# Last x tile of each later chunk turned by the DMA queue, and values, scores and global rows moved between the output steps

## The chip, the cores and the metric

The kernel runs on one core of a Trainium2 chip. The metric is device time in microseconds (us) for one execution. Engines are named as in the profile: PE is TensorE (PEld its weight loads), DVE is VectorE, ACT is ScalarE, POOL is GpSimd, SP is SyncE, whose queue issues most of the DMAs.

## The reference

Windowed attention with eight global positions, followed by a gated feed-forward layer (FFN) with a gated residual. In short:

```python
# q, k, v: (8 batches, 8 heads, 576 positions, 64); global_idx: 8 positions
scores = q @ k.T / sqrt(64)
keep   = (abs(pos_i - pos_j) <= 32) | is_global[i] | is_global[j]
attn   = softmax(where(keep, scores, -1e9))
x      = (attn @ v) laid out as 4608 tokens x 512      # heads side by side

g   = x @ w_gate                                       # 512 -> 1536
val = x @ w_val                                        # 512 -> 1536
ffn = (gelu(g) * val) @ w_out                          # 1536 -> 512
out = x + sigmoid(x @ w_res) * ffn                     # 4608 x 512, float32
```

## The kernel before

**Chunks.** The 4608 tokens are worked on as nine chunks `c` = 0 to 8 of 512 tokens. A chunk is eight attention windows of 64 queries (`CH = 8`), and its x has four tiles of 128 tokens, `t` = 0 to 3. A window sees 128 neighbouring keys and, besides, the global ones; queries that are themselves global are worked out apart, for all keys of a batch ("global rows"). A batch has nine windows, so a chunk can reach over two batches.

**One chunk's FFN.** For a chunk c > 0, PE first runs the twelve input steps (`ffn_in`, L614, through `ffn_steps`): for each of twelve blocks of 128 hidden units four matmuls into `g_ps` and four into `v_ps` (both L630), all with the turned x, `xt[c % 2]`, as the moving operand over all 512 tokens at once. ACT takes the GELU (L636), DVE multiplies (L639) into `ht`. So the first g of a chunk reads all four tiles of its turned x.

Then come sixteen output steps, `work_f`, four for each tile t (`ffn_out`): a gate (four matmuls into `r_ps`, L656, and a Tanh on ACT, L664), and three thirds of the twelve matmuls with `w_out` into `f_ps` (L686). The third one ends with `prb` on DVE (L690), `ob` on POOL (L692) and the output DMA on SP (L694). Steps are counted from 0: gate 0 is step 0, its thirds 1 to 3, gate 1 is step 4, and so on to 15.

**The next chunk's attention lies between these steps.** The order is written by hand: `jobs[n]` (L936 to L952) holds what is emitted in front of output step n, and the loop at the end of the kernel emits the jobs and then the step. Each engine and each queue keeps the order in which its instructions were emitted; waits come from the data and from the tile pools' buffers. For chunk c + 1 the jobs are:

- `global_exp` (step 0) and `global_rows` (step 4): the exponentials of the global scores on ACT, then matmuls into `sn` (L507, L510) and their masking into `vgs` on DVE (L514). Chunk 8 has none of this, since its batch, the last, was dealt with for chunk 7.
- `scores` in two halves, `half(0)` at step 1 and `half(1)` at step 4: 32 small matmuls (L534) on 64 rows of the array, four exponentials on ACT (L541) into `pt`; the masks on DVE (L557) are emitted at steps 1, 6 and 7.
- `values(c + 1, t)` at steps 5, 7, 9 and 11: sixteen matmuls with `pt` into `nd` (L575), two or four more for the global keys (L587), then on DVE a reciprocal `rden` (L599) and a product (L600) that writes x as tokens, `xtok`.
- `turn_x(c + 1, t)` at steps 7, 9, 11 and 13, in front of the step's other jobs: it turns one tile of `xtok` into `xt`. For chunks from 2 on, tiles 0 to 2 go by a DMA that transposes, issued on SP (L606); tile 3 goes by four matmuls with an identity into a PSUM tile `tx` (L610) and a copy by DVE (L611). Chunks 0 and 1 turn all tiles on PE.

**PSUM.** Three pools share its eight banks: `psm` with four buffers of a bank (g, v, r, f and half of the scores), `pss` with two (the other half of the scores, `tx`, turned globals), and `psn` with one buffer of two banks, which `sg` (global scores), `sn` and every `nd` use in turn.

**Queues.** SP's own order in these steps, before the change, is out 0, turn 0, out 1, turn 1, turn 2, out 2, out 3, and then for the next chunk the transposes of queries and keys. POOL issues the loads of queries, keys and values of later batches between its `ob`.

Of the kernel before, what the change touches and what calls it, by code (L numbers as in the profile page):

```python
# [16 lines left out]
def view(t, p0, pn, off, dims):  # L17

    step = t.ap[0][0]
    return bass.AP(tensor=t.tensor, offset=t.offset + p0 * step + off, ap=[[step, pn]] + dims)  # L20
# [3 lines left out]
def kernel(  # L24
# [460 lines left out]
    def global_exp(b, sg, ss):  # L485
        e = b % 2
        to = ptg[e].rearrange("k c r -> k (c r)")
        done = 0
        for part in ss:
            n = part.shape[1]  # L490
            nc.scalar.activation(to[:, done:done + n], part, ACTF.Exp, bias=0.0, scale=SCALE)
            done += n
        g = gt[e][:, 64:64 + S]
        nc.scalar.activation(g.rearrange("p (a c) -> p a c", a=2), sg[:, :, 0:288], ACTF.Exp, bias=0.0, scale=SCALE)
        nc.vector.tensor_tensor(g, g, maskr, ALU.mult)

    def global_rows(b):

        e = b % 2
        if b:  # L500
            sn = psn.tile([128, 2, 512], F32, name="sn", tag="nd")[:, 0, 0:2 * VG]
        else:
            sn = pss.tile([128, 2 * VG], F32, name="sn", tag="sc")
        for c in range(-1, 5):
            for p in range(NP):
                if c < 0:
                    nc.tensor.matmul(sn[32 * p:32 * p + 32, :], own[e][:, 32 * p:32 * p + 32],  # L507
                                     view(vgb, 0, 128, (b // 2) * VG, [[0, 2], [1, VG]]), start=True, stop=False)
                else:
                    nc.tensor.matmul(sn[32 * p:32 * p + 16, :], ptg[e][:, c, 16 * p:16 * p + 16],  # L510
                                     ve[e][:, c, 2 * p:2 * p + 2, :], start=False, stop=(c == 4))
        n = NP if b else NP // 2
        for p in range(0, NP, n):
            nc.vector.tensor_tensor(view(vgs, 0, 128, e * H * VG + 2 * VG * p, [[2 * VG, n], [VG, 2], [1, VG]]),  # L514
                                    view(sn, 0, 128, 0, [[0, n], [VG, 2], [1, VG]]),
                                    view(head8, 0, 128, 2 * p, [[2, n], [1, 2], [0, VG]]), ALU.mult)
# [27 lines left out]
    def scores(c, quad, pps=(0, 1)):  # L544

        i0 = (CH * c + 4 * quad) % NW
        banks = []
        for pp in pps:
            pool, tag = (psm, "mm") if pp else (pss, "sc")
            sc = [pool.tile([128, 2, 4, 64], F32, name="sc", tag=tag) for _ in range(2)]  # L550
            heads(c, quad, pp, sc, True)
            banks += [(pp, u, sc[u]) for u in range(2)]
        mine = [weigh(quad, *which, stay=(c == 1)) for which in banks]

        def mask(n0, n1):
            for m, x in mine[n0:n1]:
                nc.vector.tensor_tensor(m, x, view(maskw, 0, 128, 64 * i0, [[0, 2], [64, 4], [1, 64]]), ALU.mult)  # L557
        return mask

    def split(c, t):  # L560
        return c == 0 and t % 2 == 0

    def local_values(c, t):
        if split(c, t):
            nds = [psm.tile([128, 512], F32, name=f"nd{hf}", tag="mm") for hf in range(2)]
            nd = None
        else:
            nd = psn.tile([128, 2, 512], F32, name="nd", tag="nd")
            nds = [nd[:, 0, :], nd[:, 1, :]]
        wins = [divmod(CH * c + 2 * t + e, NW) for e in range(2)]  # L570
        for h in range(H):
            for e, (b, i) in enumerate(wins):
                vw = ve[b % 2][:, i // 2, h, :] if i % 2 == 0 else vo[b % 2][:, i // 2, h, :]
                c0 = (h * CH + 2 * t + e) * 128 - 64 * e
                nc.tensor.matmul(nds[h // 4][:, VG * (h % 4):VG * (h % 4) + VG],  # L575
                                 view(pt, 0, 128, c0, [[1, 128]]), vw, start=(h % 4 == 0 and e == 0), stop=False)
        return nd, nds, wins

    def values(c, t, begun=None):
        nd, nds, wins = begun or local_values(c, t)  # L580
        if wins[0][0] == wins[1][0]:
            parts = [(wins[0][0], 64 + 64 * wins[0][1])]
        else:
            parts = [(wins[0][0], S), (wins[1][0], 0)]
        for hf in range(2):
            for n, (b, c0) in enumerate(parts):
                nc.tensor.matmul(nds[hf][:, 0:HV], gt[b % 2][:, c0:c0 + 128], vgs[:, b % 2, HV * hf:HV * hf + HV],  # L587
                                 start=False, stop=(n == len(parts) - 1))
        rden = work.tile([128, H], F32, name="rden", tag="rden")
        if split(c, t):  # L590
            for hf in range(2):
                num = nds[hf][:, 0:HV].rearrange("p (h e) -> p h e", e=VG)
                nc.vector.reciprocal(rden[:, 4 * hf:4 * hf + 4], num[:, :, D])
                nc.vector.tensor_tensor(xtok[0][:, t, 256 * hf:256 * hf + 256].rearrange("p (h d) -> p h d", d=D),
                                        num[:, :, 0:D], view(rden, 0, 128, 4 * hf, [[1, 4], [0, D]]), ALU.mult)
            return
        num = nd[:, :, 0:HV].rearrange("p a (h e) -> p a h e", e=VG)
        r2 = rden.rearrange("p (a h) -> p a h", a=2)
        nc.vector.reciprocal(r2, num[:, :, :, D])  # L599
        nc.vector.tensor_tensor(xtok[c % 2][:, t, :].rearrange("p (a h d) -> p a h d", a=2, d=D),  # L600
                                num[:, :, :, 0:D], view(rden, 0, 128, 0, [[4, 2], [1, 4], [0, D]]), ALU.mult)

    def turn_x(c, t):
        mine = xt[c % 2][:, :, 128 * t:128 * t + 128]
        if c > 1 and t < 3:
            nc.sync.dma_start(mine, xtok[c % 2][:, t, :], transpose=True)  # L606
            return
        tx = pss.tile([128, NKT, 128], BF16, name="tx", tag="sc")
        for kk in range(NKT):
            nc.tensor.transpose(tx[:, kk, :], xtok[c % 2][:, t, 128 * kk:128 * kk + 128], ident)  # L610
        (nc.vector.tensor_copy if c or t == 3 else nc.scalar.copy)(mine, tx)  # L611
# [175 lines left out]

    values(0, 2)
    turn_x(0, 0)
    values(0, 3)  # L790
    turn_x(0, 1)
    begin(0, (0,))
    turn_x(0, 2)
    begin(0, (1,))
    begin(1)
# [11 lines left out]
    for c in range(NCH):  # L807
        b = c + 1
# [127 lines left out]
        jobs = {n: [] for n in range(16)}  # L936
        if c + 1 < NCH:
            if held is not None:
                jobs[0].append(lambda: global_exp(b, *held))
                jobs[4].append(lambda: global_rows(b))  # L940
            held_mask = {}

            def half(quad):
                held_mask[quad] = scores(c + 1, quad)

            jobs[1] += [lambda: half(0), lambda: held_mask[0](0, 4)]
            for t in range(4):
                jobs[5 + 2 * t].append(lambda t=t: values(c + 1, t))
                jobs[7 + 2 * t].insert(0, lambda t=t: turn_x(c + 1, t))
            jobs[4].append(lambda: half(1))  # L950
            jobs[6].append(lambda: held_mask[1](0, 2))
            jobs[7].append(lambda: held_mask[1](2, 4))  # L952
        for n in range(16):
# [32 lines left out]
```

The softmax here doesn't subtract the row's maximum and nothing guards it: scores larger than these inputs give would overflow.

## Time and profile before

| what | value |
|---|---|
| median of nine runs | 393.72 us (392.8 to 394.08) |
| the profiled execution's own time | 394.26 us |
| its span | 392.6 us |
| PE busy | 375.9 us, 96% of the span |
| DVE, ACT, POOL busy | 201.8, 170.2, 168.9 us |
| turns of x: by PE (L610) | 60 matmuls, 15 tiles |
| turns of x: by DMA (L606) | 21 transposes, 2.5 us from issue to landing at the median |

The profile shows one execution. A row of the timeline has the start in us from the span's start, the time from the first start to the last end, the engine, the line and the operation, the tile written and those read, the shapes, and how many instructions were merged; in square brackets stands how long the engine had been idle before it and what ended that. The ends of matmuls are modelled, and rows of PE overlap for that reason, so starts are compared. A few matmul records are missing, so a count can be one or two short. Landing is the time from a DMA's issue to its completion.

### The profile page before, as it was taken

To read this page: it belongs to the slowest core of one execution; us is meant where nothing else is said; L and a number is where in the kernel's file an instruction comes from. 1 tells how busy PE (TensorE), PEld (TensorE's weight loads), DVE (VectorE), ACT (ScalarE), POOL (GpSimd) and SP (SyncE) were. 2 spreads that over 40 slices of the span, in tenths; PEclk is the share of its full clock that TensorE was granted. 3 is DMA by queue.
4 is the path that set the end of the run, shared out by engine and by line. 5 is a ranking of instruction groups with operands and counts; after the bars stand their busy time and mean duration, and the time that the engine had idled before them with its cause. 6 is when DMAs were issued, how large, how long until landed. Compare 5 with 4: busy or idle time off the path is not lost.

```text
span 392.6 us, 8440 instructions
## 1 busy us (share of the span) xinstructions
PE 375.9 (96%) x3309; PEld 197.0 (50%) x3360; DVE 201.8 (51%) x446; ACT 170.2 (43%) x285; POOL 168.9 (43%) x203
## 2 busy tenths in 40 slices
PE   3989989999999999999999999999999999999996
PEld 2674555444644465445544554455445544554444
DVE  7766684436543664357444644655445534453422
ACT  6753783436333633354235533462338233723321
POOL 7787674858255424561466127712501210121012
PEclk9999999999999999999999999999999999999999
DMA  8999999699859913997299929993980210041002
GB/s 246 228 375 363 246 315 212 161 184 156 110 101 153 187 42 108 123 201 84 85 140 183 102 82 129 186 106 93 117 145 29 68 55 0 2 91 59 0 28 81
DMA packets 153002, 52.78 MB, mean 134 GB/s; under 512 B 136386, under 2 KB 143426, under 8 KB 152962
## 3 DMA queue, kind: packets, MB, share of 16 engines
q1 hardware_dynamic: 77024, 41.88, 44.2%
q0 software_dynamic: 75392, 9.84, 43.6%
q8 instruction: 26, 0.43, 0.5%
q10 hardware_dynamic: 546, 0.52, 0.4%
q14 instruction: 14, 0.11, 0.1%
HBM read 39.19 MB, written 9.44 MB: 124 GB/s over the span
## 4 chain that ended last, share of the span: by engine, by line
PE 71%; DMA 16%; POOL 4%; SPq 3%; issue 2%; DVE 2%; ACT 1%; ACTq 0%; DVEq 0%; POOLq 0%
PE f_ps L686 21%; PE v_ps L630 16%; PE g_ps L630 16%; PE r_ps L656 7%; PE nd L575 4%; DMA extra<-in_moe_w_val_dram 3%; SPq L185 2%; PE nd L587 2%; DMA wo_t<-in_k_dram 2%; PE sc L534 2%; DMA xt<-in_moe_w_gate_dram 2%; DMA xtok<-in_v_dram 2%; DMA kt<-k_st 2%; POOL ob L692 2%; DMA ht<-in_q_dram 2%
## 5 line engine op out<-in xcount | busy, mean ns | idle before, releaser
L639 DVE SCALAR_TENSOR_TENSOR ht<-gsb,v_ps 128x512 bf16<-128x512 bf16 x108 | 74.1, 687 | 94.9 <-PE v_ps L630 90.4
L636 ACT ACTIVATE gsb<-g_ps 128x512 bf16<-128x512 f32 x108 | 64.4, 597 | 122.7 <-PE g_ps L630 118.1
L692 POOL TENSOR_TENSOR ob<-prb,xtok 128x512 f32<-128x512 f32 x35 | 40.2, 1153 | 172.5 <-DVE prb L690 172.5
L630 PE MATMUL v_ps<-xt,wv_t 128*128 128x512 bf16 (+1 forms) x448 | 111.3, 368 | 0.7
L630 PE MATMUL g_ps<-xt,wg_t 128*128 128x512 bf16 (+1 forms) x445 | 110.7, 368 | 0.5
L686 PE MATMUL f_ps<-wo_t,ht 128*128 128x512 bf16 x402 | 96.6, 379 | 0.7
L630 PEld LDWEIGHTS <-wv_t 128*128 128x128 bf16 x456 | 43.5, 98 | 49.3 <-issue 0.4
L630 PEld LDWEIGHTS <-wg_t 128*128 128x128 bf16 x456 | 43.3, 98 | 49.4 <-issue 1.2
L686 PEld LDWEIGHTS <-ht 128*128 128x128 bf16 x420 | 40.0, 98 | 39.5
L664 ACT ACTIVATE rsb<-r_ps 128x512 bf16<-128x512 f32 x36 | 21.8, 608 | 67.0 <-PE r_ps L656 67.0
L690 DVE SCALAR_TENSOR_TENSOR prb<-rsb,f_ps 128x512 f32<-128x512 bf16 x35 | 24.0, 686 | 28.9 <-PE f_ps L686 26.4
L541 ACT ACTIVATE pt<-sc 128x512 bf16<-128x512 f32 x64 | 33.2, 619 | 9.6 <-PE sc L534 9.6
L656 PE MATMUL r_ps<-wr_t,xt 128*128 128x512 bf16 x130 | 35.6, 379 | 0.9
L91 POOL DMA_DIRECT2D q_st<-in_q_dram x25 | 21.4, 865 | 19.4 <-DMA qt<-q_st 19.1
L575 PEld LDWEIGHTS <-pt 128*128 128x128 bf16 x576 | 21.9, 97 | 9.3 <-PE r_ps L656 0.7
L557 DVE TENSOR_TENSOR pt<-pt,maskw 128x512 bf16<-128x512 bf16 x56 | 22.4, 421 | 7.1 <-ACT pt L541 5.8
L99 POOL DMA_DIRECT2D ve<-in_v_dram x30 | 25.5, 865 | 0.0
L600 DVE TENSOR_TENSOR xtok<-nd,rden 128x512 bf16<-128x512 f32 x34 | 23.5, 692 | 1.3
L575 PE MATMUL nd<-ve,pt 128*128 128x65 bf16 x320 | 22.4, 193 | 0.6 <-DVE xtok L600 0.6
L91 POOL DMA_DIRECT2D k_st<-in_k_dram x25 | 21.1, 871 | 3.6 <-DMA kt<-k_st 2.6
L599 DVE RECIPROCAL rden<-nd 128x8 f32<-128x8 f32 x34 | 7.0, 207 | 29.3 <-PE nd L587 29.3
L575 PE MATMUL nd<-vo,pt 128*128 128x65 bf16 x256 | 19.8, 193 | 0.4 <-PE r_ps L656 0.3
(174 smaller groups left out, 300.7 us busy)
## 6 DMA issues: line engine op xcount, KB each, us to landing
out_dram<-ob SPq DMA_DIRECT2D x35, 256.0 KB, 2.1
vo<-ve SPq DMA_DIRECT2D x12, 260.0 KB, 5.5
q_st<-in_q_dram POOLq DMA_DIRECT2D x20, 128.0 KB, 5.6
k_st<-in_k_dram POOLq DMA_DIRECT2D x20, 128.0 KB, 6.6
ve<-in_v_dram POOLq DMA_DIRECT2D x18, 128.0 KB, 6.5
wo_t<-in_k_dram SPq DMA_DIRECT2D x8, 256.0 KB, 6.6
vraw<-in_q_dram SPq DMA_DIRECT2D x8, 256.0 KB, 6.7
extra<-in_moe_w_out_dram SPq DMA_DIRECT2D x4, 512.0 KB, 6.9
```

The costliest lines, as they stand in the source:

```text
L91: nc.gpsimd.dma_start(dst[0:n, r, :].rearrange("p (h d) -> p h d", d=D), src[b].rearrange("h s d -> s h d")[128 * r:128 * r + n])
L99: nc.gpsimd.dma_start(t[p0:p1, c, :, 0:D], v[b].rearrange("h s d -> s h d")[s0 + p0:s0 + p1])
L541: nc.scalar.activation(sc if stay else mine, sc, ACTF.Exp, bias=0.0, scale=SCALE)
L575: nc.tensor.matmul(nds[h // 4][:, VG * (h % 4):VG * (h % 4) + VG], view(pt, 0, 128, c0, [[1, 128]]), vw, start=(h % 4 == 0 and e == 0), st ...
L600: nc.vector.tensor_tensor(xtok[c % 2][:, t, :].rearrange("p (a h d) -> p a h d", a=2, d=D), num[:, :, :, 0:D], view(rden, 0, 128, 0, [[4, ...
L630: nc.tensor.matmul(held[what][:, c0:c1], w[:, kk, 128 * j:128 * j + 128], x[:, kk, c0:c1], start=(kk == 0), stop=(kk == NKT - 1))
L636: nc.scalar.activation(held["s"], held["g"], ACTF.Gelu, bias=0.0, scale=1.0)
L639: nc.vector.scalar_tensor_tensor(ht[:, j, :], held["s"], 0.5, held["v"], ALU.mult, ALU.mult)
L656: nc.tensor.matmul(r_ps, xt[c % 2][:, kk, 128 * t:128 * t + 128], wr_t[:, kk, :], start=(kk == 0), stop=(kk == NKT - 1))
L686: nc.tensor.matmul(held["f"], ht[:, j, 128 * t:128 * t + 128], wo_t[:, j, :], start=(j == 0), stop=(j == NFF - 1))
L690: nc.vector.scalar_tensor_tensor(prb, held["r"], 1.0, held["f"], ALU.add, ALU.mult)
L692: nc.gpsimd.tensor_tensor(ob, prb, xtok[c % 2][:, t, :], ALU.add)
```

## The change

The last tile of x is turned by the DMA queue as well (for chunks from 2 on), and each turn is emitted right behind the values that it reads instead of in front of a later step. Values of tiles 0, 1 and 2 stay at steps 5, 7 and 9; those of tile 3 go from step 11 to step 10. The second half of the scores goes from step 4 to step 5, where it now stands behind the values and the turn of tile 0. The global rows go from step 4 to step 3.

```diff
     def turn_x(c, t):
         mine = xt[c % 2][:, :, 128 * t:128 * t + 128]
-        if c > 1 and t < 3:
+        if c > 1:
             nc.sync.dma_start(mine, xtok[c % 2][:, t, :], transpose=True)
             return
...
                 jobs[0].append(lambda: global_exp(b, *held))
-                jobs[4].append(lambda: global_rows(b))
+                jobs[3].append(lambda: global_rows(b))
...
             for t in range(4):
-                jobs[5 + 2 * t].append(lambda t=t: values(c + 1, t))
-                jobs[7 + 2 * t].insert(0, lambda t=t: turn_x(c + 1, t))
-            jobs[4].append(lambda: half(1))
+                n = (5, 7, 9, 10)[t]
+                jobs[n].append(lambda t=t: values(c + 1, t))
+                jobs[n].append(lambda t=t: turn_x(c + 1, t))
+            jobs[5].append(lambda: half(1))
             jobs[6].append(lambda: held_mask[1](0, 2))
             jobs[7].append(lambda: held_mask[1](2, 4))
```

On SP the order becomes out 0, turn 0, turn 1, out 1, turn 2, turn 3, out 2, out 3.

## The prediction

> **What bounds the kernel now.** I read the page from the top: busy shares, slices, the chain that ended last.
>
> ```profile
> PE 375.9 (96%) x3309; PEld 197.0 (50%) x3360; DVE 201.8 (51%) x446; ACT 170.2 (43%) x285; POOL 168.9 (43%) x203
> PE   3989989999999999999999999999999999999996
> PE 71%; DMA 16%; POOL 4%; SPq 3%; issue 2%; DVE 2%; ACT 1%; ACTq 0%; DVEq 0%; POOLq 0%
> ```
>
> PE is busy in every slice but the first and last, and no other engine is over 51%. So each microsecond added to PE's row of instructions, or put into it as a wait, lengthens the run. Next I read the timeline of PE, and of DVE and SP, for the sixteen output steps of one chunk (c=4; the values are those of chunk 5).
>
> ```profile
> 214.97 0.81 PE L656 MATMUL r_ps<-wr_t,xt 128*128 128x512 bf16 x3
> 215.92 0.64 PE L534 MATMUL sc<-qt,kt 64*128 64x64 bf16 x32
> 216.50 2.76 PE L686 MATMUL f_ps<-wo_t,ht 128*128 128x512 bf16 x12
> 219.19 0.24 PE L507 MATMUL sn<-vgb,own 128*32 128x130 bf16 x4
> ...
> 226.45 0.61 PE L587 MATMUL nd<-vgs,gt 128*128 128x260 bf16 x4
> 226.89 1.89 PE L686 MATMUL f_ps<-wo_t,ht 128*128 128x512 bf16 x8
> ...
> 231.05 0.39 PE L610 MATMUL tx<-ident,xtok 128*128 128x128 bf16 x4
> 231.28 2.75 PE L686 MATMUL f_ps<-wo_t,ht 128*128 128x512 bf16 x12
> 233.87 1.03 PE L630 MATMUL g_ps<-xt,wg_t 128*128 128x512 bf16 x4
> ```
>
> Each group starts where the one before it hands over: twelve f matmuls from 231.28 to 233.87 are 0.216 apiece, so one third of a tile (4) is 0.86 us. Nothing in these steps waits. The ends in the second column are modelled; I use starts.
>
> ```profile
> 227.09 0.21 DVE L599 RECIPROCAL rden<-nd 128x8 f32<-128x8 f32 x1 [0.46 <-PE nd L587]
> 227.34 0.69 DVE L600 TENSOR_TENSOR xtok<-nd,rden 128x512 bf16<-128x512 f32 x1
> 229.53 0.21 DVE L599 RECIPROCAL rden<-nd 128x8 f32<-128x8 f32 x1 [1.50 <-PE nd L587]
> ```
>
> This is the drain of the value bank `nd` of tile 2: PE hands over at 226.89, rden starts 0.20 later, xtok ends at 228.03, 1.14 after the hand-over. `nd` has one buffer only (pool `psn`), so tile 3's first value matmul can't start before that.
>
> **The change part by part.** The sum is made against the profiled execution, 394.26 us (span 392.6, 1.7 outside it); the median of the nine runs is 393.72, so I carry the difference over to that.
>
> *Tile 3's turn off TensorE.* Seven chunks (c=1 to 7 prepare chunks 2 to 8) lose four tx matmuls, 231.28 - 231.05 = 0.225 us of PE each: -1.57. DVE loses seven xt copies of 0.42 us and PSUM a tx tile; both were beside PE's work (DVE then waits 2.26 us for f), so nothing.
>
> *Tile 3's values one step earlier.* Tile 2 stays at step 9, tile 3 moves from 11 to 10, so between them on PE stands one third (0.86 us) where there were two (1.73). The bank needs 1.14 us plus the way from DVE back to PE. The early part of the trace has two places where PE did wait for this bank:
>
> ```profile
> 55.93 0.69 DVE L600 TENSOR_TENSOR xtok<-nd,rden 128x512 bf16<-128x512 f32 x1
> 56.73 0.19 PE L575 MATMUL nd<-vo,pt 128*128 128x65 bf16 x1 [0.27 <-PE r_ps L656]
> ...
> 62.31 0.69 DVE L600 TENSOR_TENSOR xtok<-nd,rden 128x512 bf16<-128x512 f32 x1
> 63.15 0.19 PE L575 MATMUL nd<-vo,pt 128*128 128x65 bf16 x1
> ```
>
> 56.62 to 56.73 and 63.00 to 63.15: 0.11 and 0.15 us; I take 0.13. Then tile 3 starts 1.27 after the hand-over instead of 0.86: a new wait of 0.405 us (0.385 to 0.425). The other chunks repeat it (c=1: hand-over 105.02, xtok ends 106.16). Behind the waiting matmul stands all of PE; nobody else has work for it. Seven times: +2.8. DVE is free when tile 2 is handed over (idle 0.23 to 0.46 us before its rden), with prb of tile 1 ahead of it in both orders, so the drain isn't longer than now.
>
> *The second half of the scores from step 4, in front of the gate, to step 5, behind values of tile 0; global rows from step 4 to 3.* The amount of PE work is the same; what changes is how often neighbours have different array shapes. Gate 0 should hand over at 214.97 + 4 x 0.216 = 215.83, sc starts at 215.92; f at 219.09, sn starts at 219.19: 0.09 to 0.10 us per change of shape. Before, sn, sc and the gate follow one another: into sn, sn to sc, sc to gate, three changes. After, sn stands alone between two thirds and sc alone between values and a third: four. The way out of sn into f is not in the trace; it lies between 0 and the 0.10 of the other changes, and I take 0.10, since leaving sc costs as much as entering it. Six chunks have global rows: +0.6 (0 to 0.6).
>
> Do the moved pieces find their inputs? Global rows would start near 218.3; the last exponential that they need ends at 216.1. The values of tile 0 need vgs: DVE is through with the first masks at 219.05, so vgs ends near 219.75, values start near 220.5. The second exponentials start 0.44 after their scores and take 2.06 us; the masks that use them come behind xtok of tile 0 and of tile 1 as now, and tile 2's values start some 4 us after these scores. These cost nothing; the cover is 0.7 us and more.
>
> Chunk 8 (c=7) has no global rows, and its exponentials come late, behind a table load:
>
> ```profile
> 338.73 4.03 ACT L541 ACTIVATE pt<-sc 128x512 bf16<-128x512 f32 x8
> ...
> 339.36 1.90 DVE L557 TENSOR_TENSOR pt<-pt,maskw 128x512 bf16<-128x512 bf16 x4 [2.64 <-ACT pt L541]
> ```
>
> The last mask of the first half ends at 341.26. Values of tile 0 would now come right behind gate 1, at 340.74 instead of 341.71; their eleventh matmul needs that mask and waits some 0.33 us. Against it, now the second half's scores lose 0.10 and gate 1 0.17 us on exponentials, which goes. Net +0.06 (-0.27 to +0.35).
>
> *The queues.* SP's order was out 0, turn 0, out 1, turn 1, turn 2, out 2; it becomes out 0, turns 0 and 1, out 1, turns 2 and 3, out 2. Turn 1 no longer stands behind out 1. POOL's order does not change.
>
> ```profile
> 227.89 0.35 SPq L694 DMA_DIRECT2D out_dram<-ob  x1
> 228.34 2.62 SPq L606 DMA_TRANSPOSE xt<-xtok  x2
> ...
> DMA to landing us min/median/max: 2.4/2.5/5.0
> ```
>
> Turn 2 issues at 228.34 as turn 1 does now, 1.2 us long. Tile 3's values start near 228.16, take 0.71, and xtok ends 1.14 later, near 230.0: turn 3 issues at 230.05 and by the median lands at 232.5. The next chunk's g, its first reader, would start at 233.87 + 0.405 - 0.225 = 234.05. So the landing has 4.0 us from its issue; 2.5 fits, and this step costs nothing. Without that cover, at 5.0, it costs 1.0 in that chunk. Out 2 has its ob near 232.6 and isn't held up. SP's next key and query loads hang on out 3, which moves with PE.
>
> Here the Trainium skill speaks against the change. In VectorE: DVE Perf Modes, sections "The three transpose paths" and "Rules for kernel authors", it says to turn a 128x128 block on TensorE where PSUM will do as the destination, and gives 390 ns for that and 1309 ns for the crossbar DMA. By its figure four blocks one behind the other would land 5.2 us after issue, an estimate by which seven chunks would wait about 1.2 us each and the run would come to 404. The trace disagrees on both: four blocks are 0.225 us of PE, and all four land 2.4 to 2.5 us after issue at the median.
>
> *Sum.* c=1 to 6: 0.405 - 0.225 + 0.10 = 0.28, times 6 is 1.7. c=7: 0.405 - 0.225 + 0.06 = 0.24. Together +1.9: 396.2 for an execution like the profiled one, 395.6 on the median.
>
> **The rivals.** *Late landings on top.* Of the 19 landings of x tiles that the trace can tell, three took 4.0 us or more, one 5.0. Two of these already touch the next chunk's start: at 274.46 and 354.53 its first g comes 0.1 and 0.05 us late, just behind a turn's landing at 274.32 and 354.40. A tile turned 0.3 to 0.5 later has less room. One such landing in seven chunks adds up to 1.0, two add 2: 396.6 to 397.6, here 396.9. For it: those rows. Against it: 16 of 19 land with over a microsecond left.
>
> *The bank wait is short, and the run gets faster.* All hangs on tile 3's wait, w: the sum is 7w - 1.57 + 0.6 + 0.06, zero at w = 0.13 us. If PE were free to go on (w = 0), the run would be 0.9 faster, 392.8. For it: 0.225 us of PE is certainly gone in each chunk, and no row of this stage shows a wait for the bank. Against it: the drain of 1.14 is read in every chunk, and one third is 0.86.
>
> *In between.* With w from 0.02 to 0.24 the result stays within 0.2% (0.8 us, about what a measurement of this kernel can tell from no change); the like follows if leaving sn is free and later waits take something up. PE's waits after 93 us that could do this (0.2 for kt at 214.85, those before g) are some 0.6 together: 395.0 at least, so that alone does not reach it. Middle 394.2.
>
> **How the numbers follow.** Forecast 0.65, late landings 0.18, in between 0.10, faster 0.07. The first two are slower: 0.83. Predicted: 395.6. Bounds: w at 0.385, no cost for leaving sn and the low end of c=7 give +0.8 to +1.1, so 394.6 below; late landings in one or two chunks 397.2 above. That leaves out the faster case, most of the one in between and a tail of the late one.
>
> **What the changed profile would show.** L610 with 32 matmuls instead of 60, L606 with 28 transposes instead of 21. In each chunk, PE idle some 0.4 us before the first nd of tile 3, put down to DVE xtok; tx gone between gate 3 and f; sn between two groups of f, with some 0.1 us on either side; turn 3 issued about 4 us before the next g. The prediction is wrong if PE goes from the third to tile 3's nd without a gap, if g waits for L606 in most chunks, or if tile 0's values wait for vgs.

## The result, and the profile after

The changed kernel takes 395.12 us at the median of nine runs (394.57 to 395.39). The kernel before has a median of 393.72 over the 29 runs it is compared with. The ratio is 1.0035, with a 95% interval from 1.0026 to 1.0043: slower by 1.0 to 1.7 us. The profiled execution took 395.16 us, 393.4 of it the span.

The page of the changed kernel, with the lines that were read first on the page before:

```profile
PE 375.9 (96%) x3281; PEld 195.0 (50%) x3332; DVE 199.7 (51%) x439; ACT 171.2 (44%) x285; POOL 168.5 (43%) x203
PE   3989989999999999999999999999999999999996
PE 91%; DVE 4%; ACT 2%; issue 2%; POOL 0%; DVEq 0%; POOLq 0%; ACTq 0%
```

PE lost 28 instructions, and its busy time is the same to a tenth of a microsecond; this view hides both the gain and the loss, since the modelled ends of matmuls cover a part of each wait. On the chain that ended last DVE now has 4%, where it had 2%. The timeline of PE over the same sixteen output steps as before (c=4) shows where:

```profile
216.94 1.90 PE L686 MATMUL f_ps<-wo_t,ht 128*128 128x512 bf16 x8
218.77 0.24 PE L507 MATMUL sn<-vgb,own 128*32 128x130 bf16 x4
218.84 0.46 PE L510 MATMUL sn<-ve,ptg 128*16 128x130 bf16 x20
219.45 0.81 PE L686 MATMUL f_ps<-wo_t,ht 128*128 128x512 bf16 x3 [0.16 <-issue]
...
221.77 0.64 PE L534 MATMUL sc<-qt,kt 64*128 64x64 bf16 x32
222.34 1.90 PE L686 MATMUL f_ps<-wo_t,ht 128*128 128x512 bf16 x7
...
227.44 1.02 PE L686 MATMUL f_ps<-wo_t,ht 128*128 128x512 bf16 x3
228.63 0.20 PE L575 MATMUL nd<-vo,pt 128*128 128x65 bf16 x1 [0.16 <-DVE xtok L600]
...
231.08 1.03 PE L656 MATMUL r_ps<-wr_t,xt 128*128 128x512 bf16 x4
231.94 2.75 PE L686 MATMUL f_ps<-wo_t,ht 128*128 128x512 bf16 x12
234.53 1.03 PE L630 MATMUL g_ps<-xt,wg_t 128*128 128x512 bf16 x4
```

Three things stand here. Between gate 3 and the last thirds nothing is left: 231.08 + 0.86 = 231.94, the tx group has gone. The third in front of tile 3's values starts at 227.44 and would hand over at 228.30; the first nd starts at 228.63, so PE stood still for 0.33 us, and the row names DVE's xtok. (The 0.16 in the bracket is the idle time behind the modelled end of the last matmul.) And sn now stands between two groups of f, sc between values and f. (The f group behind sn shows three of its four matmuls; gate 1 follows at 220.10, and four times 0.216 back from there the group began near 219.24, so most of the idle time in its row is the missing record.)

DVE in the same window:

```profile
227.64 0.21 DVE L599 RECIPROCAL rden<-nd 128x8 f32<-128x8 f32 x1 [0.46 <-PE nd L587]
227.89 0.69 DVE L600 TENSOR_TENSOR xtok<-nd,rden 128x512 bf16<-128x512 f32 x1
229.55 0.21 DVE L599 RECIPROCAL rden<-nd 128x8 f32<-128x8 f32 x1 [0.97 <-PE nd L587]
```

The drain of tile 2 ends at 228.58, 1.14 us after the hand-over at 227.44, as before; PE goes on 0.05 us later. SP, and the landings of all turns:

```profile
222.84 4.30 SPq L606 DMA_TRANSPOSE xt<-xtok  x2
228.45 0.35 SPq L694 DMA_DIRECT2D out_dram<-ob  x1
228.91 2.90 SPq L606 DMA_TRANSPOSE xt<-xtok  x2
...
DMA to landing us min/median/max: 2.4/2.4/4.0
```

Turn 1 no longer stands behind out 1. Turns 2 and 3 are out of SP at 231.81, 2.7 us before the next g at 234.53, which starts right where f hands over. Turn 3 was issued at 230.55 and landed at 233.34, 1.2 us before that g; in the other chunks the margin is 1.5 to 1.6. In no chunk of this execution does g wait for a turn.

### The profile page after: what moved, and what is told of

Read it like the earlier page. It is cut to its first block, busy times and chain, and to the rows that moved or that the text cites. A ratio compares the mean times of both kernels' runs of the same rounds, so it can differ in the third digit from the quotient of the medians.

```text
span 393.4 us, 8394 instructions
## 1 busy us (share of the span) xinstructions
PE 375.9 (96%) x3281; PEld 195.0 (50%) x3332; DVE 199.7 (51%) x439; ACT 171.2 (44%) x285; POOL 168.5 (43%) x203
## 4 chain that ended last, share of the span: by engine, by line
PE 91%; DVE 4%; ACT 2%; issue 2%; POOL 0%; DVEq 0%; POOLq 0%; ACTq 0%
PE g_ps L630 24%; PE v_ps L630 23%; PE f_ps L686 21%; PE r_ps L656 8%; PE nd L575 5%; PE sc L534 3%; PE nd L587 2%; DVE xtok L600 1%; PE ss L481 1%; PE sg L472 1%; PE sc L523 1%; PE tk L451 1%; PE tq L451 1%; ACT pt L541 1%; PE sn L510 1%
## 5 line engine op out<-in xcount | busy, mean ns | idle before, releaser
L630 PE MATMUL v_ps<-xt,wv_t 128*128 128x512 bf16 (+1 forms) x441 | 110.0, 367 | 0.5
L686 PE MATMUL f_ps<-wo_t,ht 128*128 128x512 bf16 x396 | 97.6, 379 | 1.9 <-issue 1.0
L686 PEld LDWEIGHTS <-ht 128*128 128x128 bf16 x420 | 39.2, 98 | 40.6
L557 DVE TENSOR_TENSOR pt<-pt,maskw 128x512 bf16<-128x512 bf16 x56 | 23.2, 424 | 7.7 <-ACT pt L541 5.8
L656 PEld LDWEIGHTS <-xt 128*128 128x128 bf16 x144 | 13.5, 97 | 15.8 <-issue 0.7
```

The costliest lines, as they stand in the source:

```text
L630: nc.tensor.matmul(held[what][:, c0:c1], w[:, kk, 128 * j:128 * j + 128], x[:, kk, c0:c1], start=(kk == 0), stop=(kk == NKT - 1))
L656: nc.tensor.matmul(r_ps, xt[c % 2][:, kk, 128 * t:128 * t + 128], wr_t[:, kk, :], start=(kk == 0), stop=(kk == NKT - 1))
L686: nc.tensor.matmul(held["f"], ht[:, j, 128 * t:128 * t + 128], wo_t[:, j, :], start=(j == 0), stop=(j == NFF - 1))
```

## The experiments

All compare with runs of the kernel before on the same chip: median 393.57 us for values_back_at_11, values_at_10_only, turn_only_at_11 and turn_only_at_13, 394.29 for the other four. Theory A is the one of the prediction, with the wait at the 0.33 us that the changed kernel's trace has; B and C are rivals: that late landings cost, or that the moved scores do.

Whole runs scatter by a microsecond and more, so for small terms a second measure is of use: the time on PE from the first sn of one chunk to the first sn of the next, which holds exactly one chunk's work. The rows for c=1 and c=2, the first that lie between output steps, before:

```profile
97.54 0.24 PE L507 MATMUL sn<-vgb,own 128*32 128x130 bf16 x4
...
137.91 0.24 PE L507 MATMUL sn<-vgb,own 128*32 128x130 bf16 x4
```

and in the changed kernel:

```profile
96.67 0.24 PE L507 MATMUL sn<-vgb,own 128*32 128x130 bf16 x4
...
137.26 0.24 PE L507 MATMUL sn<-vgb,own 128*32 128x130 bf16 x4
```

That is 40.37 and 40.59 us: +0.22 a chunk. It is one chunk of one execution. In the changed kernel the next ones take 40.92, 40.59, 40.92 and 40.59 (every other chunk has four small matmuls more); in the kernel before 40.70, 40.58, 40.70 and 40.48, two of them longer by other waits of 0.20 and 0.11 us. The same two rows in each experiment:

| kernel | sn to sn, us | against before | from the terms -0.225, +0.33, +0.10 |
|---|---|---|---|
| before | 40.37 | | |
| changed | 40.59 | +0.22 | all three: +0.21 |
| values_back_at_11 | 40.25 | -0.12 | -0.225 + 0.10 = -0.12 |
| turn_only_at_11 | 40.35 | -0.02 | -0.225, and a wait for a landing |
| values_at_10_only | 40.70 | +0.33 | +0.33 |
| turn_only_at_13 | 42.06 | +1.69 | -0.225, and a wait for a landing |
| scores_back_at_4 | 40.48 | +0.11 | -0.225 + 0.33 = +0.11 |
| scores_moved_only | 40.48 | +0.11 | +0.10 |
| short_drain_of_tile_2 | 40.33 | -0.04 | -0.225 + 0.06 + 0.10 = -0.06 |
| turn_next_to_values_at_11 | 40.14 | -0.23 | -0.225 |

**Values of tile 3 back at step 11.**

```diff
-                n = (5, 7, 9, 10)[t]
+                n = (5, 7, 9, 11)[t]
```

> The changed kernel with one thing undone: values and turn of tile 3 emitted at step 11 again (two thirds between the values of tile 2 and of tile 3), all else as changed. Theory A (the change costs by the wait of tile 3's values for the single nd buffer): that wait, 0.33 us in each of seven chunks in the changed kernel's trace, goes, so 395.1 - 2.3 = 392.8, no PE idle before tile 3's nd; the turn of tile 3 is issued about 3.2 us before the next g, and lands in time at 2.45. Theory B (the time is lost because tile 3's turn lands late at the next g, or in DMA traffic): the turn is issued 0.5 us later against g than in the changed kernel, so no gain, 395.1 or more. Theory C (moving scores and global rows is what costs): unchanged, 395.1.

Measured: 392.54 us, ratio 0.9972 (0.9960 to 0.9984). One number undone turns the change from slower into faster, as theory A had it; B and C expected 395.1. PE in this kernel:

```profile
226.68 1.89 PE L686 MATMUL f_ps<-wo_t,ht 128*128 128x512 bf16 x8
...
228.89 0.39 PE L587 MATMUL nd<-vgs,gt 128*128 128x260 bf16 x2
...
230.84 2.75 PE L686 MATMUL f_ps<-wo_t,ht 128*128 128x512 bf16 x12
233.43 0.38 PE L630 MATMUL g_ps<-xt,wg_t 128*128 128x512 bf16 x1
```

Eight f matmuls stand between the two tiles' values. They hand over at 228.41, and the global part of tile 3's values, 0.48 us of work later, starts at 228.89: no gap. Nor is there one before g at 233.43.

**Tile 3's values moved, and nothing else.**

```diff
-                jobs[5 + 2 * t].append(lambda t=t: values(c + 1, t))
+                jobs[(5, 7, 9, 10)[t]].append(lambda t=t: values(c + 1, t))
```

(on the kernel before)

> The kernel before with only tile 3's values moved from step 11 to step 10; tile 3 is still turned on PE in front of step 13, and scores and global rows stay. It measures the wait for the nd buffer by itself. Theory A: 7 x 0.33 = 2.3 more, 396.0, with 0.33 us of PE idle before tile 3's nd, put down to DVE xtok. Theories B and C: no turn and no scores are moved, so 393.7.

Measured: 395.89 us, ratio 1.0057 (1.0039 to 1.0075). The wait is there with no DMA turn and no moved scores:

```profile
228.02 1.02 PE L686 MATMUL f_ps<-wo_t,ht 128*128 128x512 bf16 x4
229.21 0.20 PE L575 MATMUL nd<-vo,pt 128*128 128x65 bf16 x1 [0.17 <-DVE xtok L600]
```

228.02 + 0.86 = 228.88, and the first nd starts 0.33 later. It does so in all seven chunks, 0.33 each time.

**The same wait with a shorter drain.** This one shows that it is the drain that PE waits for, and not tile 3's own inputs.

```diff
+        na = 1 if c > 1 and t == 2 else 2
-        nc.vector.tensor_tensor(xtok[c % 2][:, t, :].rearrange("p (a h d) -> p a h d", a=2, d=D),
-                                num[:, :, :, 0:D], view(rden, 0, 128, 0, [[4, 2], [1, 4], [0, D]]), ALU.mult)
+        nc.vector.tensor_tensor(xtok[c % 2][:, t, :].rearrange("p (a h d) -> p a h d", a=2, d=D)[:, 0:na],
+                                num[:, 0:na, :, 0:D], view(rden, 0, 128, 0, [[4, na], [1, 4], [0, D]]), ALU.mult)
```

(on the changed kernel)

> The changed kernel, but for chunks from 2 on the product that drains tile 2's values covers only the first four heads; the other half of that tile's x keeps what an earlier chunk left there, so part of the computation is left out. The drain gets shorter by 0.69 - 0.42 = 0.27 us. Theory A (tile 3's values wait for the drain of the single nd buffer): the wait falls from 0.33 to about 0.06 in each of seven chunks, 395.1 - 1.9 = 393.2. Rival (tile 3's values wait for something else, such as their own exponentials or masks): unchanged, 395.1, with 0.33 us still idle before them.

This kernel leaves out half of tile 2's product. Measured: 393.38 us, ratio 0.9970 (0.9957 to 0.9982). DVE's product takes 0.42 us instead of 0.69:

```profile
227.81 0.21 DVE L599 RECIPROCAL rden<-nd 128x8 f32<-128x8 f32 x1 [0.46 <-PE nd L587]
228.06 0.42 DVE L601 TENSOR_TENSOR xtok<-nd,rden 128x256 bf16<-128x256 f32 x1
```

and PE goes on at once when it ends:

```profile
227.62 1.02 PE L687 MATMUL f_ps<-wo_t,ht 128*128 128x512 bf16 x4
228.54 0.20 PE L575 MATMUL nd<-vo,pt 128*128 128x65 bf16 x1
```

228.54 - 228.48 = 0.06 behind xtok; the wait is 228.54 - (227.62 + 0.86) = 0.06 us, as theory A expected.

**Only the turn, right behind its values.**

```diff
-        if c > 1 and t < 3:
+        if c > 1:
...
-                jobs[7 + 2 * t].insert(0, lambda t=t: turn_x(c + 1, t))
+                if t < 3:
+                    jobs[7 + 2 * t].insert(0, lambda t=t: turn_x(c + 1, t))
+                else:
+                    jobs[11].append(lambda: turn_x(c + 1, 3))
```

(on the kernel before)

> The kernel before with only tile 3's turn given to the DMA queue, emitted right behind its values at step 11; values, scores, global rows and the other turns stay where they were. Theory A: only the 0.225 us of tx per chunk goes, 393.7 - 1.6 = 392.1; but the three turns 1, 2, 3 now stand in a row on SP behind out 1, 1.3 us of issue each, so turn 3 is issued near 231.0 in the chunk whose g starts at 233.65: 0.2 us to spare at the median landing, so a few late ones may give back up to 0.5: 392.1 to 392.7. Theory B (landing is what costs): g waits in most chunks, 393.7 or more. Theory C: 392.1.

Measured: 393.18 us, ratio 0.9989 (0.9975 to 1.0002), not told apart from no change: most of the expected 1.6 us is missing, and the 0.5 allowed for late landings was too little. SP shows the three turns in a row behind out 1:

```profile
227.03 0.35 SPq L694 DMA_DIRECT2D out_dram<-ob  x1
227.47 4.32 SPq L606 DMA_TRANSPOSE xt<-xtok  x3
```

The third one's issue starts at 230.59, and PE waits for a landing:

```profile
230.18 2.75 PE L686 MATMUL f_ps<-wo_t,ht 128*128 128x512 bf16 x12
233.18 1.02 PE L630 MATMUL g_ps<-xt,wg_t 128*128 128x512 bf16 x4 [0.24 <-DMA xt<-xtok]
```

f hands over at 232.77, so g stands for 0.40 us here; five other chunks lose 0.13 to 0.24, one nothing, 1.4 us in sum. In all seven, turn 3 is issued only 2.6 to 2.7 us before g starts; in the changed kernel it was 4.0. The mechanism is theory B's, but of another place: not the turn as such, but its being the third on the queue.

**Only the turn, where TensorE's turn stood.**

```diff
-        if c > 1 and t < 3:
+        if c > 1:
```

(on the kernel before; the turn is emitted in front of step 13)

> The kernel before with only the condition changed: tile 3's turn is a DMA, emitted where the PE turn stood, in front of step 13, which on SP is behind out 2. Theory A: it waits on SP for ob of tile 2 (out 2 issued near 232.4 in the chunk whose g starts at 233.65), is issued near 232.8 and lands near 235.3, so g waits 1.7 us in each of seven chunks: +12 - 1.6, about 404. Rival (the place of the turn does not matter since it is hidden): 392.1.

Measured: 404.91 us, ratio 1.0283 (1.0259 to 1.0306). On SP the turn comes behind out 2:

```profile
237.24 0.34 SPq L694 DMA_DIRECT2D out_dram<-ob  x1
237.68 1.22 SPq L606 DMA_TRANSPOSE xt<-xtok  x1
```

and PE's g waits for it from 238.44 on:

```profile
235.85 2.75 PE L686 MATMUL f_ps<-wo_t,ht 128*128 128x512 bf16 x12
240.22 1.02 PE L630 MATMUL g_ps<-xt,wg_t 128*128 128x512 bf16 x4 [1.61 <-DMA xt<-xtok]
```

1.78 us in this chunk, 1.78 to 1.92 in all seven, 12.9 in sum; less 1.6 that is 11.3, as measured. So what hides a turn is its place on the queue, not its being a DMA.

**Scores and global rows moved, and nothing else.**

```diff
-                jobs[4].append(lambda: global_rows(b))
+                jobs[3].append(lambda: global_rows(b))
...
-            jobs[4].append(lambda: half(1))
+            jobs[5].append(lambda: half(1))
```

(on the kernel before)

> The kernel before with only the second half of the scores moved to step 5 behind values of tile 0 and the global rows to step 3; tile 3 stays on PE and its values at step 11. Theory A: 6 x 0.10 = 0.6 above the kernel before, about 394.2, and nothing else in the trace. Rival (free): 393.6. Rival (most of the cost): 395.

Measured: 394.11 us, ratio 0.9998 (0.9984 to 1.0012). By whole runs this is not told apart from no change, and theory A's +0.6 us (1.0015) lies just outside the interval (more on that reference under the last experiment). The trace does show the 0.1 us in each chunk:

```profile
217.90 0.24 PE L507 MATMUL sn<-vgb,own 128*32 128x130 bf16 x4
217.97 0.45 PE L510 MATMUL sn<-ve,ptg 128*16 128x130 bf16 x20
218.35 1.04 PE L686 MATMUL f_ps<-wo_t,ht 128*128 128x512 bf16 x4
219.23 1.03 PE L656 MATMUL r_ps<-wr_t,xt 128*128 128x512 bf16 x4
...
220.57 0.39 PE L587 MATMUL nd<-vgs,gt 128*128 128x260 bf16 x2
220.90 0.64 PE L534 MATMUL sc<-qt,kt 64*128 64x64 bf16 x32
```

The two global matmuls of the values take 0.11 each, so they hand over at 220.80, and sc starts 0.10 later: a change of shape that was not there. Moving these pieces is a small loss at most, not the cost of the change.

**The changed kernel with scores and global rows back at step 4.** The same two lines, the other way round.

> The changed kernel with the second half of the scores and the global rows back at step 4 (sn, sc and gate 1 next to each other again), values and turns as changed. Theory A: one change of the array's shape less in six chunks, 0.10 us each, so 0.6 below the changed kernel: about 394.5, or 0.9 above the kernel before of the same call. Rival (moving the scores is most of the cost): back to 393.6 or below. Rival (the moves of scores and rows are free): 395.1.

Measured: 394.21 us, ratio 1.0009 (0.9992 to 1.0026); theory A's +0.9 (1.0023) is within the interval, but so is no change. The chunk of 40.48 us, 0.11 less than in the changed kernel, agrees with A.

**What remains when the losses are left out.** Turns by DMA right behind their values, values at 5, 7, 9 and 11, scores and rows at step 4.

```diff
-                n = (5, 7, 9, 10)[t]
+                n = (5, 7, 9, 11)[t]
...
-                jobs[3].append(lambda: global_rows(b))
+                jobs[4].append(lambda: global_rows(b))
...
-            jobs[5].append(lambda: half(1))
+            jobs[4].append(lambda: half(1))
```

(on the changed kernel)

> Every turn by DMA right behind its values as in the changed kernel, but values of tile 3 at step 11, scores and global rows at step 4: only the gain is kept. Theory A: 7 x 0.225 = 1.6 below the kernel before, 392.0, 0.6 below the same kernel with moved scores (392.5); turn 1 is issued ahead of out 1, so turn 3 is not the third in a row on SP and g waits for no landing. Rival (the waits for landings eat it, as where turns 1 to 3 stand in a row): 393.2.

Measured: 391.89 us, ratio 0.9933 (0.9916 to 0.9950): faster than both kernels. It differs from "only the turn, right behind its values" in the place of turns 0 to 2 alone:

```profile
221.80 3.62 SPq L606 DMA_TRANSPOSE xt<-xtok  x2
226.74 0.34 SPq L694 DMA_DIRECT2D out_dram<-ob  x1
227.19 4.08 SPq L606 DMA_TRANSPOSE xt<-xtok  x2
```

Turn 1 is out before out 1, so turn 3 is the second behind it and not the third. One g of seven waited for a landing, 0.19 us; in the other six chunks turn 3 landed 0.7 us before g. By the medians the gain is 2.4 us, more than 7 x 0.225 = 1.6. A part can be the waits for landings that the profiled execution of the kernel before has and this one has not, 0.11 and 0.27 us where g waits for turn 2:

```profile
274.46 1.02 PE L630 MATMUL g_ps<-xt,wg_t 128*128 128x512 bf16 x4
...
354.53 1.02 PE L630 MATMUL g_ps<-xt,wg_t 128*128 128x512 bf16 x3
```

(The twelve f matmuls in front of them start at 271.76 and 351.67 and hand over at 274.35 and 354.26.) Another part may be the reference. All four kernels that are compared with the median of 394.29 come out 0.4 to 1.0 us lower against it than theory A has them, the one with the scores alone too, in which no turn moved; against 393.6, near the other two medians of the kernel before (393.57 and 393.72), all four would lie within 0.3 us of what was expected. A reference that is high by chance would explain that; it is not shown. The sn to sn times do not rest on it.

## Why the prediction was right

The forecast was +1.9 us on the median, the change is +1.4 (1.0 to 1.7). By its own steps:

- *Tile 3's turn off TensorE, 0.225 us a chunk:* right. Kept alone, it shortens a chunk by 0.23.
- *Tile 3's values one step earlier, a wait for the single nd buffer:* the mechanism was right, and it is the one that decides: without it the same change is faster than the kernel before. The size was off. It was put at 0.405 us a chunk and measured 0.33. Of its two parts the drain of 1.14 us was exact; the way back from DVE to PE was put at 0.13, from two rows early in the trace, and is 0.05 to 0.06. Seven times 0.08 is 0.5 us, as much as the difference between 1.9 and 1.4. The right size stood in the trace before: of the two rows used, one is put down to PE's r_ps and one to nothing, but a third, earlier one names DVE's xtok, whose end at 22.47 is 0.06 us ahead of it:

```profile
21.78 0.69 DVE L600 TENSOR_TENSOR xtok<-nd,rden 128x512 bf16<-128x512 f32 x1
22.53 0.20 PE L575 MATMUL nd<-ve,pt 128*128 128x65 bf16 x1 [0.56 <-DVE xtok L600]
```

- *Scores and global rows, one more change of shape in six chunks, 0.10 us each:* right in the trace of the run with the scores alone. The change out of sn into f, which could not be read before, can be read there: five groups of sn matmuls, 0.056 us apart in the records, take 217.97 to 218.25, and f starts at 218.35. Whole runs could not show it.
- *Chunk 8 (c=7):* the eleventh value matmul of tile 0 was to wait some 0.33 us for the last mask, against 0.27 that goes. It was the eleventh, and it waited 0.25:

```profile
342.02 0.19 PE L575 MATMUL nd<-ve,pt 128*128 128x65 bf16 x1
342.31 0.20 PE L575 MATMUL nd<-vo,pt 128*128 128x65 bf16 x1
```

- *The queues:* right. Turn 3 goes out about 4.0 us before the next g (230.55 and 234.53), and no g waited.
- *Sum from the measured terms:* c=1 to 6 0.22 each, c=7 0.33 - 0.225 - 0.02 = 0.08, together 1.4. That this meets the difference of the medians to a tenth is partly luck. From the first g of c=2 (112.00 before, 112.21 after) to the first g of c=8 (354.53 and 355.36) the two profiled executions differ by 0.62 us, where these terms give 1.18; the rest, 0.56, is about what the kernel before lost there in three waits that the changed one did not have, 0.20 at 214.85 and the 0.11 and 0.27 in front of g. Whether every execution of the kernel before has them is not known.

The rival of late landings did not come about in the changed kernel, but the two runs with the turn alone show what it hangs on: with turn 3 third in the row, issued 1.3 to 1.4 us later against g, g waits in six chunks of seven, and behind out 2 it costs 12.9 us. The rows given for this rival were read in part wrongly: only the landing in front of 274.46 was slow, 3.96 us. In front of 354.53 turn 2 took 2.75 us and was issued late, at 351.64, behind turn 1; and that g came 0.27 us late, not 0.05. The Trainium skill's rule, in VectorE: DVE Perf Modes, "Rules for kernel authors", to turn a 128x128 block on TensorE where PSUM will do, does not hold for this kernel: PE is the bound, and with the last turn given to the DMA queue and every turn right behind its values the run is 0.5 to 0.8% shorter, of which tile 3's turn itself, 7 x 0.225, is 1.6 us, or 0.4%.

The Trainium skill's Perfetto Trace Analysis, "Optimization Strategy", says that the same gap repeating on the engine that should be saturated can mean too little PSUM for the next tile. Here it was so: seven gaps of 0.33 us, and one buffer for nd, which PE went back into as soon as DVE had read it. No run gave nd a second buffer.

## What to carry to other kernels

Where one PSUM buffer is filled, drained and filled again, the work between two fills must be longer than the drain with its hand-overs (here 1.19 us); moving the fill one step earlier cost 0.33 us a chunk, more than the 0.225 that the turn gave. A transfer that takes over work from the bound engine pays only if its place on its queue lets it land before the first reader: the same turn was worth 1.6 us or cost 11. A change that bundles several moves should be taken apart, since the good one (the turn next to its values) was hidden by a bad one.

## What had not been expected of the hardware

- The way back from the end of DVE's read to PE's first matmul into the freed bank was 0.05 to 0.06 us in all the runs with this wait. The two early rows that the prediction used had 0.11 and 0.15; why they are longer was not settled.
- Three turns that were ready together left SP 1.3 us apart (turn_only_at_11), so a row of them adds that much to the last one's landing for each one ahead.
